# Spectral filter and squared-ReLU layer on one core: seven products for the first group too, a casting load of W_out, and batch 1's filter products moved to slots 12 to 28

## The chip, the cores and the metric

The kernel runs on one core of a Trainium2 chip. A core has TensorE (PE, the matmuls; PEld is its weight load), VectorE (DVE), ScalarE (ACT), GpSimd (POOL) and SyncE (SP), and each runs its own instructions in the order in which the program gives them. Transfers are queued by SP (hardware queue) and by POOL (software queue) and done by 16 DMA engines. The metric is the device time of a whole execution in microseconds, as the median of several runs; the profile is of one execution and has a span of its own, which lies some 2 to 3 us under the measured time.

## The reference, cut to what matters

```python
X = np.fft.rfft(x, axis=1)                       # x: (8, 3008, 256) float32
Y = X * (filt_r + 1j * filt_i)[None]             # filters: (1505, 256)
y = np.fft.irfft(Y, n=3008, axis=1).astype(np.float32)
t = y.reshape(8 * 3008, 256)                     # 24064 tokens
h = np.maximum(t @ w_in, 0.0)                    # w_in: (256, 2048)
return (h * h @ w_out).astype(np.float32)        # w_out: (2048, 256)
```

## The kernel before

The transform is done as matmuls, batch by batch, with two passes through DRAM (`dU` after the first stage, `dZ` after the inverse's first stage). The tokens are worked off in 47 groups of 512. A group takes eight **slots**; in slot s = 8g + k the kernel does one eighth of group g's first matmul (`ffn_g1`, ReLU on ScalarE, square on VectorE) and one eighth of the second matmul of group g - 1. The transform of later batches is laid into the slots by a plan.

The loop, and the plan for batch 1 (the transform of batch 0 is done ahead of the loop, and so is `unit_a` of batch 1):

```python
    for s in range((NG + 1) * SLOTS):
        g, k = divmod(s, SLOTS)
        if g < NG:
            ffn_g1(g, k)                      # 4 matmuls of 512 columns, ReLU
        run(work, s, 0)                       # the plan, first half of the slot
        if 10 <= s < 14:
            make_t(s - 10)                    # sums of blocks of W_out, VectorE
        if (s - 1) // SLOTS - 1 in SEVEN:     # before: groups 1 to 45
            products((s - 1) // SLOTS - 1, (s - 1) % SLOTS)
        if g > 0 and g - 1 not in SEVEN:      # before: groups 0 and 46
            ffn_g2(g - 1, k)                  # 8 matmuls of 256 columns
        run(work, s, 1)
        ...                                   # [cut: ffn_out]
        if g - 1 in SEVEN:
            sums(g - 1, k)                    # VectorE, for k = 0, 1, 2, 4
        if g < NG:
            ffn_sq(g, k)                      # VectorE, every second slot

    # in the plan, for b == 1 (f = 0):
        for k in range(4):
            moves.append(((4.5, 5.5, 7.5, 7.5)[k], cast_wout, k, nc.vector))
        moves.append((0, read_u, b))
        ...                                   # [cut]
        for p in range(12):
            r = 8 + 20 * p / 11 if b == 1 else ...
            units.append((f + r, unit_b, b, p))
            if b == 1 and 2 <= p < 10:
                moves.append((f + r, load_x, 2, p - 2))
            units.append((f + r + (4.5 if b == 1 else ...), unit_p, b, p))
```

The second matmul comes in two forms. `ffn_g2` is the plain one: 64 matmuls of 256 columns a group. `products` splits the matrices into 2 x 2 blocks and takes seven block products in place of eight: 112 matmuls of 128 columns a group, for which VectorE makes four sums of blocks of the squared h (`sums`), and four sums of blocks of W_out once (`make_t`); ScalarE copies four results out and VectorE adds three times.

```python
    def make_t(k):            # b11 .. b22: blocks of sWout
        i0, i1 = ((b12, b11), (b22, t[:, 0]), (b22, b12), (b21, t[:, 1]))[k]
        nc.vector.tensor_sub(out=t[:, k], in0=i0, in1=i1)

    def unit_b(b, p):         # forward transform of two classes, times the filter
        ps = psF(...)                         # a PSUM tag of two buffers
        for i in range(2):
            nc.tensor.matmul(ps[:, i * D:(i + 1) * D], sSB[:, 2 * p + i, :],
                             uts[b][:, 2 * p + i, :], start=True, stop=True)
        nc.vector.tensor_mul(out=prod, in0=..., in1=sF[:, :, 2 * p:2 * p + 2, :])
        for i in range(2):                    # second half added by DMA
            nc.gpsimd.dma_start(out=prod[64 * i:64 * i + 64, 0],
                                in_=prod[64 - 64 * i:128 - 64 * i, 1], accum_op=add)
```

W_out is loaded in float32 through the SP queue between the first two z tiles, into a tile of the two-buffer pool `p_h2`, which the h tiles of the groups use as well; VectorE casts it in four parts in slots 4 to 7. Ahead of the loop:

```python
    read_z(0, 0)
    load_wout(0)          # 1 MB each, nc.sync.dma_start
    read_z(0, 1)
    load_wout(1)
    for c in range(4):
        unit_a(1, c)      # ends in two writes of dU through SP
    for n in range(4):
        unit_y(0, n)      # needs z tile 0
    read_z(0, 2)
```

Of the kernel before, what the change touches and what calls it, by code (L numbers as in the profile page):

```python
# [9 lines left out]
F16 = mybir.dt.float16  # L10
F32 = mybir.dt.float32
# [99 lines left out]
def kernel(  # L111
# [9 lines left out]
    nc = tc.nc  # L121
# [3 lines left out]
    NJT = DFF // 128  # L125
    assert S == N1 * N2 and NF == S // 2 + 1 and D == 256 and DFF == 2048
    T = B * S
    NG = T // TG
# [8 lines left out]
    const = ctx.enter_context(tc.tile_pool(name="const", bufs=1))  # L137
# [9 lines left out]
    p_h2 = ctx.enter_context(tc.tile_pool(name="p_h2", bufs=2))  # L147
# [152 lines left out]

    sWin = const.tile([128, 2, DFF], F16, name="sWin")
    sWout = const.tile([128, NJT, 256], F16, name="sWout")
    w32s = {}

    def load_win():

# [12 lines left out]
    wins = []  # L319

    def load_wout(k):
        if k == 0:
            w32s[2] = p_h2.tile([128, NJT, 256], F32, tag="h2", name="wout32")
        c = slice(8 * k, 8 * k + 8)
        nc.sync.dma_start(out=w32s[2][:, c, :],
                          in_=moe_w_out.rearrange("(jt r) c -> r jt c", r=128)[:, c, :])

    def cast_wout(k, eng):
        c = slice(4 * k, 4 * k + 4)
        eng.tensor_copy(out=sWout[:, c, :], in_=w32s[2][:, c, :])  # L330


    def write_u(b, c):
# [144 lines left out]
    ztiles = [const.tile([112, 8, D], F16, name=f"zt_{c}") for c in range(2)]  # L478
# [3 lines left out]
    def read_z(b, c, ks=(0, 1)):  # L482
        zt = ztiles[c % 2]
        v = dZ[b].rearrange("(q j) d -> q j d", j=NM)
        for k in ks:
            nc.sync.dma_start(out=zt[64 * k:64 * k + 48],
                              in_=v[48 * k:48 * k + 48, 8 * c:8 * c + 8, :])
        zts[(b, c)] = zt
# [29 lines left out]
    def ffn_g1(g, s):  # L518
        if s == 0:
            h2s[g] = p_h2.tile([128, NJT, TG], F16, tag="h2", name=f"h2_{g}")  # L520
        h2 = h2s[g]
        ps = psH(f"psH_{g}_{s}")
        segs = []
        t = g * TG
        while t < (g + 1) * TG:
            b, r = divmod(t, S)
            n = min((g + 1) * TG - t, S - r)
            segs.append((t - g * TG, b, r, n))
            t += n
        for i in range(2):  # L530
            jt = 2 * s + i
            for o, b, r, n in segs:
                for dt in range(2):
                    nc.tensor.matmul(ps[:, i, o:o + n],  # L534
                                     sWin[:, dt, jt * 128:(jt + 1) * 128],
                                     yts[b][:, dt, r:r + n],
                                     start=(dt == 0), stop=(dt == 1))
        nc.scalar.activation(out=h2[:, 2 * s:2 * s + 2, :], in_=ps, func=AF.Relu)  # L538
# [8 lines left out]
    def ffn_g2(g, s):  # L547
        t, half = divmod(s, 2)
        if s % 4 == 0:
            pso[g] = psO(f"psO_{g}_{s}")  # L550
        elif g == NG - 1 and half == 0:
            pso[g] = psF(f"psO_{g}_{s}").rearrange("p (a d) -> p a d", d=256)
        for jt in range(8 * half, 8 * half + 8):
            nc.tensor.matmul(pso[g][:, t % 2, :], h2s[g][:, jt, t * 128:(t + 1) * 128],  # L554
                             sWout[:, jt, :], start=(jt == 0), stop=(jt == NJT - 1))
# [36 lines left out]
    def make_t(k):  # L592

        w = sWout.rearrange("p (q e) c -> p q e c", e=2)
        b11, b12 = w[:, :, 0, 0:128], w[:, :, 0, 128:256]
        b21, b22 = w[:, :, 1, 0:128], w[:, :, 1, 128:256]
        if k == 0:
            sg["t"] = p_t.tile([128, 4, 8, 128], F16, tag="t", name="sT")
        t = sg["t"]
        i0, i1 = ((b12, b11), (b22, t[:, 0]), (b22, b12), (b21, t[:, 1]))[k]  # L600
        nc.vector.tensor_sub(out=t[:, k], in0=i0, in1=i1)
        sg["w"] = {1: b11, 2: b21, 3: b22, 4: t[:, 3], 5: t[:, 0], 6: t[:, 1], 7: t[:, 2]}
# [70 lines left out]
    def fft_plan():  # L673

        fixed, units, moves = [], [], []
        for b in range(1, B):
            f = (b * S // TG) * SLOTS - (48 if b > 1 else 40)
            d = 0
            if b == 1:
                for n in range(4, 16):  # L680
                    fixed.append(((n if n < 8 else n + 2 if n < 12 else 2 * n - 7) + n % 2 / 2,
                                  unit_y, 0, n))
                moves.append((7.5, read_z, 0, 3))
                for k in range(4):
                    moves.append(((4.5, 5.5, 7.5, 7.5)[k], cast_wout, k, nc.vector))
                moves.append((0, read_u, b))
                d = 7
            else:
                for a in range(16):
                    if a % 2 == 0 and b > 2:  # L690
                        moves.append((f + ((-57 + 2.3 * a) if b == 3 else (-66 + 2.75 * a)),
                                      load_x, b, a // 2))
                    if a % 4 == 3:
                        units.append((f + ((-13, -9, -5.5, -3)[a // 4], -46 + 2.1 * a, -56 + 2.75 * a)[min(b, 4) - 2],
                                      unit_a, b, a // 4))
                moves.append((f + (2 if b == 2 else -6.5), read_u, b))
            for p in range(12):
                r = 8 + 20 * p / 11 if b == 1 else 6 + 28 * p / 11 if b == 2 else -2 + 36 * p / 11
                units.append((f + r, unit_b, b, p))
                if b == 1 and 2 <= p < 10:  # L700
                    moves.append((f + r, load_x, 2, p - 2))
                units.append((f + r + (4.5 if b == 1 else 7 - 2.5 * p / 11), unit_p, b, p))
            for c in range(4):
                moves.append((f + (40 + d / 14, 43, 48, 54)[c] - d, read_z, b, c))
            for n in range(16):
                (fixed if n < 4 else units).append((f + YN[n] - d, unit_y, b, n))
        work, used, done = {}, set(), {}
        for r, *u in fixed:
            h = int(2 * r)
            used.add(h)  # L710
            work.setdefault(h, []).append(u)
        rank = (unit_a, unit_b, unit_p, unit_y)
        for r, *u in sorted(units, key=lambda u: (rank.index(u[1]), u[0])):
            after = done.get((u[0], u[1]), -1)
            if u[0] is unit_a:
                h = min((h for h in range(max(2 * int(r) - 2, after + 1), 2 * int(r) + 12)
                         if h % 2 == 0 and not used & {h - 1, h, h + 1}),
                        key=lambda h: abs(h - 2 * r))
                used |= {h - 1, h, h + 1}
                done[(u[0], u[1])] = h  # L720
                work.setdefault(h, []).append(u)
                continue
            early = 1 if u[0] is unit_b else 3
            h = min((h for h in range(max(int(2 * r) - early, after + 1), int(2 * r) + 12)
                     if h not in used),
                    key=lambda h: (sum(h + i in used for i in (-2, -1, 1, 2)) > 2) * 2
                    + abs(h - int(2 * r)))
            used.add(h)
            done[(u[0], u[1])] = h
            work.setdefault(h, []).append(u)  # L730
        for r, *u in moves:
            work.setdefault(int(2 * r), []).append(u)
        return work

    def run(plan, s, place):
        for f, *a in plan.get(2 * s + place, ()):
            f(*a)
# [10 lines left out]
    for k in range(2):  # L748
        c = slice(12 * k, 12 * k + 12)
# [24 lines left out]
    for k in range(6):  # L774
        if k % 3 == 0:
            sSPx.append(p_u.tile([128, 12, 128], F16, tag="u", name=f"sSPx_{k}"))
        c, o = slice(4 * k, 4 * k + 4), slice(4 * k % 12, 4 * k % 12 + 4)
# [6 lines left out]
    for k in range(7):  # L784
# [7 lines left out]
        if k < 4:  # L792
            place_f(0, k + 2, nc.scalar)
    read_z(0, 0)
    load_wout(0)
    read_z(0, 1)
    load_wout(1)
    for c in range(4):
        unit_a(1, c)
    for n in range(4):  # L800
# [1 line left out]
    prologue[0] = False  # L802
    read_z(0, 2)

    SEVEN = range(1, NG - 1)
    work = fft_plan()

    for s in range((NG + 1) * SLOTS):
        g, k = divmod(s, SLOTS)
        if g < NG:  # L810
            ffn_g1(g, k)
        run(work, s, 0)
        if 10 <= s < 14:
            make_t(s - 10)
        if (s - 1) // SLOTS - 1 in SEVEN:
            products((s - 1) // SLOTS - 1, (s - 1) % SLOTS)
        if g > 0 and g - 1 not in SEVEN:
            ffn_g2(g - 1, k)
        run(work, s, 1)
        if g > 0 and g - 1 not in SEVEN:  # L820
            ffn_out(g - 1, k)
        if g - 1 in SEVEN:
            sums(g - 1, k)
        if g < NG:
            ffn_sq(g, k)
# [30 lines left out]
```

## Time and profile before

| what | value |
|---|---|
| time, median of 3 runs | 764.76 us (764.64 to 764.91) |
| span of the profiled execution | 761.6 us |
| TensorE busy | 741.7 us, 97% of the span |
| VectorE busy | 653.3 us, 86% |
| ScalarE busy | 564.5 us, 74% |
| TensorE idle, 0 to 50 us / 50 to 76 us / 76 to 700 us | 8.5 / 5.1 / 2.8 us |

The last row is what matters for this change: it is read from the busy time of TensorE in these stretches. The loop of slots begins near 50 us. A wait is found in the table of who waited for whom, and its place in the timeline of the engine. Busy times of one instruction on VectorE overlap a little: the elementwise operations of 1.22 us follow one another at 1.13 to 1.15 us, so sums over a stretch are taken from start to start.

### The profile page before, as it was taken

How to read it: one execution, taken by the hardware profiler on the slowest of the kernel's cores; microseconds unless marked ns; L12 is line 12 of the kernel's file. 1: busy time of each engine (PE TensorE's matmuls, PEld its weight loads, DVE VectorE, ACT ScalarE, POOL GpSimd, SP SyncE). 2: the span in 40 equal slices, each digit the busy share in tenths (PEclk: the TensorE clock that was granted, in tenths of full speed). 3: DMA queues.
4: the chain of work that ended last, by engine and by line, in shares of the span. 5: the costliest groups of instructions: out<-in, count | busy, mean ns of one | idle time of the engine just before them, and what ended most of it. 6: DMA issues, size and time to landing. Idle time of an engine off the chain costs nothing.

```text
span 761.6 us, 19875 instructions
## 1 busy us (share of the span) xinstructions
PE 741.7 (97%) x8358; PEld 542.3 (71%) x8358; DVE 653.3 (86%) x727; ACT 564.5 (74%) x801; POOL 191.6 (25%) x264
## 2 busy tenths in 40 slices
PE   8977999999999999999999999999999999999998
PEld 5834766777777777877678776787767777777776
DVE  5856987899899998998979999899989989888783
ACT  3965788778877777777777877777777777777773
POOL 3802540143312331233212324033311222000000
PEclk9999999999999999999999999999999999999999
DMA  9986787665776556654585655775546334321011
GB/s 365 300 235 197 126 165 195 181 134 118 151 198 146 104 119 172 184 120 102 125 213 135 123 117 114 199 153 107 110 119 194 90 71 98 97 79 48 29 57 56
DMA packets 103025, 107.54 MB, mean 141 GB/s; under 512 B 10144, under 2 KB 93472, under 8 KB 101400
## 3 DMA queue, kind: packets, MB, share of 16 engines
q1 hardware_dynamic: 85576, 84.09, 36.4%
q0 software_dynamic: 17216, 22.00, 20.4%
q8 instruction: 65, 1.06, 0.6%
q10 hardware_dynamic: 144, 0.18, 0.1%
q14 instruction: 24, 0.20, 0.1%
HBM read 57.97 MB, written 48.23 MB: 139 GB/s over the span
## 4 chain that ended last, share of the span: by engine, by line
PE 87%; DMA 6%; DVE 3%; ACT 2%; SPq 1%; issue 1%; POOL 0%; DVEq 0%; ACTq 0%
PE psH L534 39%; PE psX L647 20%; PE psY L647 15%; PE psY L504 3%; PE psB L423 2%; PE psP L468 2%; DMA f<-in_filt_i_dram 2%; PE psO L554 2%; PE psA L355 2%; DVE prod L431 1%; SPq L338 1%; DMA zt<-dZ 1%; DMA prod<-prod 1%; DMA dZ<-ze 1%; DVE h L545 1%
## 5 line engine op out<-in xcount | busy, mean ns | idle before, releaser
L538 ACT ACTIVATE h<-psH 128x1024 f16<-128x1024 f32 x376 | 385.5, 1026 | 167.8 <-PE psH L534 164.0
L534 PE MATMUL psH<-yt,sWin 128*128 128x512 f16 (+7 forms) x1728 | 388.0, 352 | 1.2 <-ACT h L538 0.5
L545 DVE TENSOR_TENSOR h<-h 128x2048 f16<-128x2048 f16 (+1 forms) x192 | 229.9, 1198 | 46.8 <-ACT h L538 46.4
L438 POOL DMA_DIRECT2D prod<-prod x168 | 138.6, 962 | 441.4 <-DVE prod L431 438.8
L534 PEld LDWEIGHTS <-sWin 128*128 128x128 f16 x1728 | 149.4, 98 | 91.3 <-issue 4.3
L647 PEld LDWEIGHTS <-sum 128*128 128x128 f16 x2880 | 177.4, 98 | 25.2 <-issue 5.3
L647 PEld LDWEIGHTS <-h 128*128 128x128 f16 x2160 | 132.6, 98 | 24.4 <-issue 5.3
L431 DVE TENSOR_TENSOR prod<-psB,sF 128x1024 f16<-128x1024 f32 x84 | 102.5, 1220 | 18.6 <-PE psB L423 17.5
L647 PE MATMUL psX<-sT,sum 128*128 128x128 f16 x1440 | 102.4, 219 | 0.0
L647 PE MATMUL psY<-sT,sum 128*128 128x128 f16 x720 | 69.7, 219 | 0.0
L195 POOL DMA_DIRECT2D x<-in_x_dram x64 | 55.3, 1030 | 2.2 <-PE psA L355 2.2
L623 DVE TENSOR_TENSOR sum<-sum,h 128x2048 f16<-128x2048 f16 x45 | 54.9, 1221 | 0.9
L647 PE MATMUL psY<-sWout,sum 128*128 128x128 f16 x720 | 54.7, 219 | 0.6 <-DVE bot L662 0.6
L647 PE MATMUL psY<-sWout,h 128*128 128x128 f16 x720 | 55.0, 219 | 0.0
L647 PE MATMUL psX<-sT,h 128*128 128x128 f16 x720 | 54.9, 219 | 0.0
L629 DVE TENSOR_TENSOR sum<-h,sum 128x2048 f16<-128x2048 f16 x45 | 54.8, 1218 | 0.0
L626 DVE TENSOR_TENSOR sum<-h 128x2048 f16<-128x2048 f16 x45 | 54.8, 1217 | 0.0
L620 DVE TENSOR_TENSOR sum<-h 128x2048 f16<-128x2048 f16 x45 | 54.7, 1215 | 0.0
L470 ACT CAST ze<-psP 128x512 f16<-128x512 f32 x84 | 49.1, 585 | 0.7 <-PE psP L468 0.4
L647 PE MATMUL psX<-sWout,h 128*128 128x128 f16 x720 | 47.6, 219 | 0.0
L504 PE MATMUL psY<-sC,zt 112*128 112x94 f16 x512 | 43.1, 207 | 3.5 <-DMA zt<-dZ 3.2
L513 DVE CAST yt<-psY 128x376 f16<-128x376 f32 x62 | 33.7, 543 | 14.2 <-PE psY L504 14.2
(75 smaller groups left out, 583.3 us busy)
## 6 DMA issues: line engine op xcount, KB each, us to landing
zt<-dZ SPq DMA_DIRECT2D x64, 192.0 KB
dU<-u SPq DMA_DIRECT2D x56, 192.0 KB
prod<-prod POOLq DMA_DIRECT2D x168, 64.0 KB, 2.7
dZ<-ze SPq DMA_DIRECT2D x28, 384.0 KB
x<-in_x_dram POOLq DMA_DIRECT2D x48, 192.0 KB, 5.0
ut<-dU SPq DMA_DIRECT2D x7, 1024.0 KB
out_dram<-top SPq DMA_DIRECT2D x31, 128.0 KB
out_dram<-bot SPq DMA_DIRECT2D x31, 128.0 KB
```

The source lines that it names most:

```text
L195: nc.gpsimd.dma_start(out=t[64 * h + p0:64 * h + p1], in_=v[p0:p1, 8 * c:8 * c + 8, :])
L431: nc.vector.tensor_mul(out=prod, in0=ps.rearrange("p (a d) -> p a d", d=D).unsqueeze(1).to_broadcast([128, 2, 2, D]), in1=sF[:, :, 2 * p:2 ...
L438: nc.gpsimd.dma_start(out=prod[64 * i:64 * i + 64, 0], in_=prod[64 - 64 * i:128 - 64 * i, 1], accum_op=mybir.AluOpType.add)
L504: nc.tensor.matmul(ps[:, 94 * jj:94 * jj + 94], zt[:, 4 * (g % 2) + jj, dt * 128:(dt + 1) * 128], sSY, start=True, stop=True)
L534: nc.tensor.matmul(ps[:, i, o:o + n], sWin[:, dt, jt * 128:(jt + 1) * 128], yts[b][:, dt, r:r + n], start=(dt == 0), stop=(dt == 1))
L538: nc.scalar.activation(out=h2[:, 2 * s:2 * s + 2, :], in_=ps, func=AF.Relu)
L545: nc.vector.tensor_mul(out=v, in0=v, in1=v)
L620: nc.vector.tensor_add(out=t, in0=a21, in1=a22)
L623: nc.vector.tensor_sub(out=t, in0=f[5], in1=a11)
L626: nc.vector.tensor_sub(out=t, in0=a11, in1=a21)
L629: nc.vector.tensor_sub(out=t, in0=a12, in1=f[6])
L647: nc.tensor.matmul(o[:, t, :], f[p][:, q, 128 * t:128 * t + 128], sg["w"][p][:, q, :], start=(m == 0 and p in (1, 2)), stop=(q == 7), skip ...
```

## The change

Four things are moved or replaced. W_out is loaded by POOL's queue with a cast to float16 in the transfer, straight into its final tile; its start is tied to the arrival of the first z tile by a one-element copy on GpSimd. The four casts on VectorE and the float32 tile go. Group 0's second matmul takes the seven products instead of the plain form, which needs the sums of W_out two slots earlier, in slots 8 to 11. Batch 1's filter products (`unit_b`, and `unit_p` and the loads of batch 2's x with them) start in slot 12 and not in slot 8, and lie closer together. The purpose is to keep the transfers that the first slots wait for free of W_out, and to give TensorE other work while batch 1's transformed rows are still under way.

```diff
     def load_wout(k):
-        if k == 0:
-            w32s[2] = p_h2.tile([128, NJT, 256], F32, tag="h2", name="wout32")
         c = slice(8 * k, 8 * k + 8)
-        nc.sync.dma_start(out=w32s[2][:, c, :],
-                          in_=moe_w_out.rearrange("(jt r) c -> r jt c", r=128)[:, c, :])
-
-    def cast_wout(k, eng):
-        c = slice(4 * k, 4 * k + 4)
-        eng.tensor_copy(out=sWout[:, c, :], in_=w32s[2][:, c, :])
+        nc.gpsimd.dma_start(out=sWout[:, c, :],
+                            in_=moe_w_out.rearrange("(jt r) c -> r jt c", r=128)[:, c, :])
@@ the plan
-                for k in range(4):
-                    moves.append(((4.5, 5.5, 7.5, 7.5)[k], cast_wout, k, nc.vector))
@@
-                r = 8 + 20 * p / 11 if b == 1 else 6 + 28 * p / 11 if b == 2 else -2 + 36 * p / 11
+                r = 12 + 16.5 * p / 11 if b == 1 else 6 + 28 * p / 11 if b == 2 else -2 + 36 * p / 11
@@ ahead of the loop
     read_z(0, 0)
-    load_wout(0)
     read_z(0, 1)
-    load_wout(1)
+    tiny = const.tile([1, 1], F16, name="tiny")
+    nc.gpsimd.tensor_copy(out=tiny, in_=ztiles[0][0:1, 0, 0:1])
+    for k in range(2):
+        load_wout(k)
@@ the loop
-    SEVEN = range(1, NG - 1)
+    SEVEN = range(NG - 1)
@@
-        if 10 <= s < 14:
-            make_t(s - 10)
+        if 8 <= s < 12:
+            make_t(s - 8)
```

More of the change, by code (lines that the diff above doesn't have):

```diff
@@ L302 @@
     sWout = const.tile([128, NJT, 256], F16, name="sWout")
-    w32s = {}
     def load_win():
```

## The prediction

> **What bounds the kernel now.** I read the page first: its shares say which engine is short of time.
>
> ```profile
> PE 741.7 (97%) x8358; PEld 542.3 (71%) x8358; DVE 653.3 (86%) x727; ACT 564.5 (74%) x801; POOL 191.6 (25%) x264
> ```
>
> TensorE is the bound over the whole; what it doesn't lose early it keeps to the end, because from 140 to 700 us it has under 1.5 us of idle time. So the change can only pay where TensorE stands still or runs slowly, and the table of who waited for whom, taken for TensorE from 40 to 130 us, names the places:
>
> ```profile
> PE psB L423 <- DMA ut<-dU: 4.1, 1, 4.1
> PE psY L504 <- DMA zt<-dZ: 3.2, 2, 2.8
> PE psA L355 <- DVE prod L431: 0.7, 1, 0.7
> ```
>
> The first is the largest wait of the whole trace: the first filter product of batch 1 waits for batch 1's rows. TensorE's timeline shows where it lies, and what follows it (start us, length us):
>
> ```profile
> 60.27 0.81 PE L534 MATMUL psH<-yt,sWin 128*128 128x512 f16 x3 [0.34 <-DVE yt L513]
> 65.15 0.61 PE L423 MATMUL psB<-ut,sSB 128*128 128x256 f16 x2 [4.08 <-DMA ut<-dU]
> 65.56 1.91 PE L554 MATMUL psO<-sWout,h 128*128 128x256 f16 x8
> ```
>
> 60.27 is slot 8. TensorE stands from 61.1 to 65.15. The SP queue says why the rows are late:
>
> ```profile
> 44.92 0.39 SPq L325 DMA_DIRECT2D wout<-in_moe_w_out_dram x1
> ...
> 46.44 0.43 SPq L325 DMA_DIRECT2D wout<-in_moe_w_out_dram x1
> 46.97 10.49 SPq L338 DMA_DIRECT2D dU<-u  x8
> 57.57 1.38 SPq L486 DMA_DIRECT2D zt<-dZ  x2
> 61.29 0.82 SPq L414 DMA_DIRECT2D ut<-dU x2
> ```
>
> The eight writes of dU take 10.49 us to issue although their data stand ready, with 2 MB of W_out queued ahead of them; only then can ut be read. The stretches around it (length, busy us of PE, PEld, DVE, ACT, POOL, granted clock, DMA share, GB/s):
>
> ```profile
> 61.10:65.15 4.05, 0.00 (x0) 0.00 (x1) 1.45 (x2) 1.02 (x1) 0.00 (x0) 0.95 0.71 231
> 65.15:68.60 3.45, 3.45 (x15) 2.05 (x16) 1.23 (x1) 0.00 (x0) 1.27 (x2) 0.56 0.93 303
> 68.60:84.30 15.70, 15.59 (x121) 10.83 (x120) 13.44 (x15) 11.54 (x15) 7.96 (x12) 1.00 0.51 85
> 84.30:107.40 23.10, 22.26 (x246) 15.92 (x246) 22.34 (x23) 18.02 (x28) 13.22 (x19) 1.00 0.83 152
> ```
>
> Two things to see. After the stall the granted clock is 0.56 for 3.45 us. And from 84.3 to 107.4 us VectorE is busy 22.34 of 23.1 us: there it has as little room as TensorE.
>
> **What the Trainium skill says.** "TensorE: Matmul & The Clock Gate", Part 1, says that after an idle window of some 3.4 us the array's clock falls to half, and needs about as long of steady work to come back. The trace agrees: 4.05 us idle, then 0.56 for 3.45 us. "DMA: Bandwidth & Descriptors", section on queues, rings and completion order, says that each DMA engine goes round robin between the queues it has work for; so W_out in POOL's queue will share with the dU writes and not stand ahead of them. The trace before can't show it for this stage. The same page, section "SWDGE vs HWDGE vs iDMA", says that a cast in a transfer goes by the software queue only; the x loads here do so (192 KB of output land in 5.0 us, median). "SBUF — State Buffer", in the "DVE blocks DMA" box, says that VectorE in a two-port mode keeps GpSimd from writing descriptors; nothing before shows whether the squares would delay W_out so.
>
> **The change part by part.**
>
> *The wait for ut.* Without W_out ahead, dU's 1.5 MB and ut's first 0.5 MB need less queueing. In the old run 44 to 60 us moved some 300 GB/s. Shared half and half with W_out, I estimate dU done near 57, ut's first part near 62 and the second near 64. The first product now stands in slot 12 to 13, near 68 us. So the 4.05 us are gone, with some 5 us in hand.
>
> *The clock.* 3.45 us at 0.56 are 1.93 us of work at full clock: 1.5 us saved, as TensorE no longer idles long enough.
>
> *Seven products for group 0.* The chain of waits has 8 plain matmuls in 0.87 us and 16 block products in 0.90 us at full clock. 64 x 0.109 = 6.96 us go, 112 x 0.056 = 6.27 us come: 0.7 us saved on TensorE. On TensorE alone the sum is 4.05 + 1.5 + 0.7 = 6.2 us.
>
> *VectorE pays.* Group 0 now needs four sums (1.15 us start to start) and three adds (0.34 us): 4.6 + 1.0 = 5.6 us, all before slot 17 and so in front of batch 1's last products. The four casts of W_out (2.7 us) go, but they lay in slots 4 to 7, where the ReLUs at 1.02 us on ScalarE set the pace; they free nothing that counts. The built order has the same 12 products up to slot 28 as before. In the old run VectorE went from 62.5 (last square of group 0) to 108.9 us (end of the twelfth product): 46.4 us, of which 7.9 idle in the rows of that stretch, 6.2 of it on those products' matmuls. That leaves 38.5 us of work. After the change it is 38.5 + 5.6 = 44.1 us, from 61.6 on (the ReLU of slot 7 ends at 60.4, the square takes 1.2). It ends at 105.7 against 108.9: **3.2 us** earlier, not 6.2.
>
> *How far TensorE may be ahead.* The twelfth product's matmul needs a buffer of the tag psF. The one two allocations before is the half of psA that VectorE copies; after that copy VectorE still has a square and two products, 3 x 1.14 = 3.4 us. So TensorE can reach it at 105.7 - 3.4 = 102.3 us against 107.4: 5.1 us earlier. The next inverse product waits for the eleventh product's buffer, which costs some 0.4 us. I take 4.7 us. From there to the end the work is the same as before, and VectorE has room again (16.53 of 20.1 us busy from 107.4 to 127.5), so the gain stays.
>
> *W_out itself.* It is first needed in slot 8 (first sum, VectorE) and slot 9 (first block product), near 61.5 us. It starts when z tile 0 is there, near 47.5. Its 2.1 MB read at half of 300 GB/s take 14 us, at the full rate 7; dU's writes finish in between, so I put its landing at 58 to 62. Some 0.3 us of expected loss.
>
> *Sum.* 764.8 - 4.7 + 0.3 = 760.4; I choose **760.3 us**, a little lower as h's second tile no longer waits for W_out's casts (1.1 us on ScalarE in slot 8, off TensorE's path before only because of the stall).
>
> **The rivals.**
>
> *A. TensorE keeps it all.* VectorE's extra 5.6 us hide, as sums are wanted only two slots after they are made. For it: TensorE is the chain from 65 to 96 us in the old run. Against it: VectorE had 96.7% from 84.3 to 107.4 us already, before anything was added. Time: 764.8 - 6.2 = 758.6.
>
> *B. W_out comes late.* If the software queue is slower than its half, sums and block products wait in order on both engines. Landing at 65 gives the old stall back under another name (sT or psX waiting for sWout), and a slow clock again. For it: W_out starts 2.6 us later than before and shares. Against it: the old run moved the same bytes by 61.3 us through one queue, W_out first. Time: 763 to 765.
>
> *C. The z tile of batch 1.* The last inverse product moves from the end of slot 32 to slot 33. In the old run z of batch 1 was read just in time: TensorE waited 0.37 us at 127.5. A later write turns part of the gain into that wait. It would cost 0.5 to 1.5 us: 761 to 762. Against it: the SP queue held that write back by stores until 121.42, while its tile was ready at 117.5, so there is room.
>
> **Range and chances.** VectorE's bound gives 3.2 to 5.1 us, TensorE's 6.2, a late W_out near 0, and the z wait takes up to 1.5. Eight in ten I put between 757.8 and 763.3. 2% are 15.3 us; no term comes near that, as TensorE has only 5.1 us idle from 50 to 76 us. So within 2% has 0.98, and each side 0.01.
>
> **What would show it.** Right: no wait of psB for ut; granted clock at 1.0 from 61 to 69 us; L325 and the cast's line gone; VectorE over 95% busy from slot 9 to slot 28, and the waits of TensorE there name it (psB, psP or psA behind prod); slot 28's products 4 to 5 us earlier. Wrong: sWout named in a wait near 61 us (B); psY waiting for zt over 1 us near 122 (C); VectorE with gaps of some us between 70 and 105 while TensorE is closed up (A). The prediction fails most if the software queue takes over 16 us for W_out, or if dU's writes stay slow to issue without it.

## The result, and the profile after

The changed kernel takes **759.2 us** (758.92 to 759.70) against 764.84 us for the kernel before on the same chip: a ratio of 0.9924, 95% interval 0.9906 to 0.9941. It is faster by about 0.8%, and lies within 2%, inside the predicted range and 1.1 us under the predicted 760.3.

The page's first lines hardly move: TensorE 741.7 to 740.7 us busy, VectorE 653.3 to 655.8. What moved is seen only in the first 130 us. Who waited for whom, TensorE, 40 to 130 us, in the changed kernel (us in total, times, longest):

```profile
PE psY L497 <- DMA zt<-dZ: 3.4, 2, 3.1
PE psB L416 <- DVE prod L424: 1.0, 1, 1.0
PE psY L640 <- DVE bot L655: 0.8, 1, 0.8
...
PE psP L461 <- DVE prod L424: 0.5, 1, 0.5
PE psY L497 <- DVE prod L424: 0.4, 2, 0.2
```

The wait of psB for ut is gone. The first line was there before; in place of the long wait stand the short ones below it, and they name VectorE. The stretches from slot 8 on (length, busy us of PE, PEld, DVE, ACT, POOL, granted clock, DMA share, GB/s) say the same:

```profile
61.00:65.00 4.00, 3.90 (x40) 2.60 (x40) 3.59 (x6) 3.06 (x5) 0.00 (x0) 1.00 0.37 99
65.00:69.00 4.00, 4.00 (x54) 3.05 (x52) 4.00 (x6) 2.78 (x4) 0.00 (x0) 1.00 1.06 402
69.00:84.00 15.00, 13.04 (x137) 9.13 (x134) 14.97 (x18) 9.35 (x15) 7.81 (x10) 1.00 0.44 81
84.00:103.00 19.00, 18.52 (x203) 13.17 (x202) 18.55 (x20) 14.85 (x23) 13.12 (x18) 1.00 0.94 160
```

TensorE works through where it stood from 61.1 to 65.15, at full clock. From 65 to 84 us VectorE is busy 18.97 of 19 us and TensorE only 17.04: the bound has passed from a transfer to VectorE. The SP queue, though, hardly changed:

```profile
45.66 10.16 SPq L331 DMA_DIRECT2D dU<-u  x8
55.93 1.74 SPq L479 DMA_DIRECT2D zt<-dZ  x2
62.56 0.82 SPq L407 DMA_DIRECT2D ut<-dU  x2
```

The dU writes still take 10.16 us to issue (10.49 before), and ut is read at 62.56 us, later than the 61.29 of before. W_out left the SP queue and the rows came no sooner. In the other nine traces with the casting load the writes took 8.5 to 9.6 us, but ut was read at 61.7 to 64.0 us, so it was never sooner than before.

In the two traces the first inverse unit of batch 1 (slot 38) starts at 127.55 us before and at 124.46 us after, 3.1 us apart:

```profile
127.55 0.33 PE L504 MATMUL psY<-sC,zt 112*128 112x94 f16 x4 [0.37 <-DMA zt<-dZ]
```

```profile
124.46 0.33 PE L497 MATMUL psY<-sC,zt 112*128 112x94 f16 x4 [0.33 <-DMA zt<-dZ]
```

Another 0.9 us is a wait of an inverse product for its addition near 364 us, which of these two only the trace before has. Together they are the 4.0 us between the spans. The medians differ by 5.6 us: the profiled execution of before took 763.72 us, 1.1 under its median, and the changed kernel's 759.70, 0.5 over. Between 200 and 700 us TensorE is idle for 0.6 to 1.9 us in five of the fourteen traces of this study and not at all in the other nine, so the traces are used for places and causes, the medians for sizes.

The wait near 364 us may not be chance. The three kernels that load W_out as before (before, e1, e3) all have it, at 0.7 to 1.1 us; of the ten with the casting load none has, but e11, which loads nothing, has 0.6 us of it. Each is one execution, and no run shows what causes it.

### The profile page after: what moved, and what is told of

The parts are those of the page before. It is cut to its first block, busy times and chain, and to the rows that moved or that the text cites. A ratio compares the mean times of both kernels' runs of the same rounds, so it can differ in the third digit from the quotient of the medians.

```text
span 757.6 us, 19976 instructions
## 1 busy us (share of the span) xinstructions
PE 740.7 (98%) x8406; PEld 542.3 (72%) x8406; DVE 655.8 (87%) x730; ACT 564.7 (75%) x803; POOL 193.9 (26%) x267
## 4 chain that ended last, share of the span: by engine, by line
PE 87%; DVE 5%; DMA 4%; ACT 2%; issue 1%; SPq 0%; DVEq 0%; ACTq 0%
PE psH L527 40%; PE psX L640 20%; PE psY L640 16%; PE psY L497 3%; PE psB L416 2%; PE psP L461 2%; DMA f<-in_filt_i_dram 2%; PE psA L348 2%; DVE prod L424 2%; ACT h L531 1%; PE psO L547 1%; DVE h L538 1%; DMA zt<-dZ 1%; DMA dZ<-ze 1%; PE psf L284 1%
## 5 line engine op out<-in xcount | busy, mean ns | idle before, releaser
L640 PEld LDWEIGHTS <-sum 128*128 128x128 f16 x2944 | 181.4, 98 | 26.2 <-issue 6.3
L640 PEld LDWEIGHTS <-h 128*128 128x128 f16 x2208 | 135.6, 98 | 24.5 <-issue 5.3
L640 PE MATMUL psX<-sT,sum 128*128 128x128 f16 x1472 | 104.7, 219 | 0.0
L619 DVE TENSOR_TENSOR sum<-h 128x2048 f16<-128x2048 f16 x46 | 56.0, 1217 | 0.0
L613 DVE TENSOR_TENSOR sum<-h 128x2048 f16<-128x2048 f16 x46 | 55.9, 1216 | 0.0
```

Source lines behind the costliest of these rows:

```text
L613: nc.vector.tensor_add(out=t, in0=a21, in1=a22)
L619: nc.vector.tensor_sub(out=t, in0=a11, in1=a21)
L640: nc.tensor.matmul(o[:, t, :], f[p][:, q, 128 * t:128 * t + 128], sg["w"][p][:, q, :], start=(m == 0 and p in (1, 2)), stop=(q == 7), skip ...
```

## The experiments

All were compared with the kernel before on their own chip.

**e1: the move alone.** The kernel before with `r = 12 + 16.5 * p / 11` for batch 1.

```diff
-                r = 8 + 20 * p / 11 if b == 1 else ...
+                r = 12 + 16.5 * p / 11 if b == 1 else ...
```

> The kernel before with one edit: batch 1's filter products from slot 12 on. My theory (the gain comes from the move, W_out's new way does nothing for the transfers of dU and ut): the wait of psB for ut (4.1 us) and the half clock after it (1.5 us) go; VectorE has only its old 38.5 us from 62.5 on and ends the twelfth product near 101 to 104, so TensorE sets the end: 5 to 5.5 us less, 759.3 to 760. Rival (W_out's way out of the SP queue is what pays): the move alone leaves most of the loss, 762 to 764.

Measured 760.23 against 764.67 us, ratio 0.9936 (0.9924 to 0.9949). The theory holds, though the time is 0.2 us above the 759.3 to 760 that it gave: one line gives 4.4 us. The wait for ut isn't in the list of waits, while ut is still read at 61.05 us. The interval overlaps that of the changed kernel (0.9906 to 0.9941). The line also packs the products closer and takes the loads of batch 2's x with it; e12 below, with the same packing from slot 11, speaks for the start as what counts.

**e2: W_out alone.** The kernel before with only the casting loads and the one-element copy. The edits shown undo the rest in the changed kernel.

```diff
-                r = 12 + 16.5 * p / 11 if b == 1 else ...
+                r = 8 + 20 * p / 11 if b == 1 else ...
-    SEVEN = range(NG - 1)
+    SEVEN = range(1, NG - 1)
-        if 8 <= s < 12:
-            make_t(s - 8)
+        if 10 <= s < 14:
+            make_t(s - 10)
```

> The kernel before with W_out by casting loads behind the first z tile, nothing else. My theory: ut still comes at 64 to 66 us as dU's writes are as slow to issue as before (10.2 us in the changed kernel against 10.5), so the wait of psB for ut stays at 4 us or a little more: 764 to 766. Rival (W_out's way pays): ut comes before slot 8, the wait goes, 759 to 761.

Measured 764.47 against 764.67 us, ratio 1.0001 (0.9993 to 1.0010): nothing. Its SP queue and TensorE's wait:

```profile
45.73 9.32 SPq L331 DMA_DIRECT2D dU<-u  x8
55.16 1.89 SPq L479 DMA_DIRECT2D zt<-dZ  x2
62.28 0.82 SPq L407 DMA_DIRECT2D ut<-dU  x2
```

```profile
PE psB L416 <- DMA ut<-dU: 4.1, 1, 4.1
```

The dU writes were issued by 55.05, 2.4 us sooner than in the kernel before, yet ut could be read only at 62.28, when their data had landed. The chains of work that ended last show the landing of the last write, first in the kernel before, then in e2:

```profile
56.51 4.70 DMA dU<-u
61.29 3.82 DMA ut<-dU
```

```profile
53.59 8.55 DMA dU<-u
62.28 3.64 DMA ut<-dU
```

The last write was issued 2.9 us earlier, took 3.9 us longer, and landed at 62.14 in place of 61.21. Out of the queue is not out of the way.

**e3: seven products for group 0 alone**, with the sums of W_out in slots 8 to 11 (the two edits that e2 undoes, made in the kernel before).

> The kernel before with seven products for group 0 and the sums of W_out in slots 8 to 11, nothing else. Theory A (VectorE is the bound from 70 to 107 us, so its 5.6 us more cost more than TensorE's 0.7 us less): 766 to 769. Theory B (TensorE is the bound, the sums hide): 764.0 to 764.5.

Measured 765.49 against 764.67 us, ratio 1.0010 (1.0001 to 1.0020): slower, though the interval only just clears 1, so theory A's direction, but by 0.8 us and not by the 1.3 to 4 it gave. The wait for ut was still there (3.6 us), and part of VectorE's extra work lay in it: VectorE was idle 2.5 us for the products' matmuls in 61 to 107 us, where the kernel before had 6.2.

**e4: the changed kernel without the seven products for group 0** (SEVEN and `make_t` undone as in e2).

> The changed kernel with the plain second matmul for group 0 and the sums of W_out back in slots 10 to 13. Theory A (VectorE bound by the sums of group 0): the twelfth product ends near 101 to 103 instead of 106.9, TensorE sets the end: 756.5 to 758.5. Theory B (TensorE bound): 0.7 us more than the changed kernel, 759.7 to 760.2.

Measured 758.73 against 764.67 us, ratio 0.9913 (0.9899 to 0.9926). Theory B had it 0.7 us above the changed kernel, and it isn't; but against 0.9924 and 0.9931 for the changed kernel on other chips the intervals overlap, so e4 alone doesn't decide. Its list of waits shows what took over:

```profile
PE psY L497 <- DMA zt<-dZ: 4.2, 2, 2.7
PE psP L461 <- DMA prod<-prod: 0.7, 1, 0.7
```

With VectorE relieved, TensorE comes to slot 38 early and waits 1.5 us there for batch 1's z (0.33 in the changed kernel). The twelfth product ended at 105.07 us, not at the 101 to 103 expected.

e4 and e1 differ only in W_out's way; e4's ratio is lower by 0.0023, with intervals that touch. By slot 38 e1 is the earlier of the two (122.96 against 123.73 us), and what e1 loses comes later: its trace has 1.9 us of waits between 200 and 700 us, one of them the wait near 364 us above, and e4's has none. Whether the casting load helps once the move is made stays open.

**e5: the changed kernel again**, for comparison on the next chip.

> The changed kernel itself, so that the others of this call are compared with it on one chip: 759.2 as before (758.9 to 759.7), the same waits.

Measured 759.41 against 764.84 us, ratio 0.9931 (0.9918 to 0.9943).

**e6: the changed kernel with the products back from slot 8.**

```diff
-                r = 12 + 16.5 * p / 11 if b == 1 else ...
+                r = 8 + 20 * p / 11 if b == 1 else ...
```

> The changed kernel with batch 1's filter products back from slot 8 on. Theory (the move is what pays): ut is read at 62.6 us in the changed kernel, so a first product in slot 8 waits for it until about 66.5; psB waits 4 to 5 us for ut, and group 0's seven products then press VectorE as well: 764.5 to 767. Rival (the three other parts pay a good share): 761 to 763.

Measured 765.65 against 764.84 us, ratio 1.0019 (1.0009 to 1.0028). Without the move the other three parts together cost 0.8 us:

```profile
PE psB L416 <- DMA ut<-dU: 4.3, 1, 4.3
PE psY L497 <- DMA zt<-dZ: 3.6, 2, 3.0
PE psY L497 <- DVE prod L424: 2.1, 2, 1.9
```

**e7: the clock.** In the changed kernel's trace the granted clock stays at half until 54 us, around the 3.1 us wait for z tile 0; in e5's trace of the same kernel it is back by 52. This version keeps TensorE busy through that wait.

```diff
-            for k in range(2):
+            for k in range(46 if n == 0 else 2):
+                k %= 2
                 nc.tensor.matmul(ps[:, 128 * k:128 * k + 128], zero, zero, start=True, stop=True)
```

> The changed kernel with 44 more zero matmuls of 128 columns in front of the first inverse unit, while TensorE waits for z tile 0 (44.6 to 47.9 us), their results overwritten. Theory: the granted clock stays at 1.0 and the first slots run at full clock, so the first ReLU comes 1.5 us earlier than 52.0 and slot 8 1 to 2 us earlier than 61.1; VectorE starts slot 8 earlier by as much: 757.2 to 758.2. Rival: W_out's arrival or the z tiles hold slot 8 at 61 anyway, and nothing is gained (759.2), or the extra matmuls delay the first unit (759.5).

Measured 759.02 us beside e5's 759.41; ratios 0.9926 (0.9914 to 0.9939) and 0.9931: not to be told apart. Yet the clock did stay up. First the stretch of the changed kernel again (e5), then of e7:

```profile
50.00:52.00 2.00, 1.98 (x7) 0.70 (x6) 0.30 (x1) 0.37 (x1) 0.00 (x0) 0.68 1.17 181
```

```profile
50.00:52.00 2.00, 1.75 (x9) 0.73 (x8) 0.00 (x0) 1.78 (x2) 0.00 (x0) 1.00 1.25 172
```

The ReLU of slot 8 starts at 59.59 us, 1.4 earlier than e5's 60.99. Then e7 waits 0.9 us for z tile 2 and VectorE 0.5 us for W_out, and 0.7 us for z in slot 38: the time went into new waits for transfers.

**e8: batch 2's x loads earlier**, on e4.

```diff
-                    moves.append((f + r, load_x, 2, p - 2))
+                    moves.append((f + 12 + (p - 2) / 2, load_x, 2, p - 2))
```

> The changed kernel with the plain second matmul for group 0 (as in e4) and with batch 2's x loads in slots 12 to 15.5, not spread between the additions by DMA up to slot 25. Theory C (with VectorE relieved, the additions queued on GpSimd behind the x loads are what TensorE waits for): the waits of psP for prod and x go, 0.5 to 1.5 us less than e4: 757.2 to 758.3. Rival (z of batch 1 at slot 38 takes the gain back, as e4's 1.5 us wait of psY for zt shows): psY waits longer instead and the time is e4's, 758.7.

Measured 760.09 against 764.84 us, ratio 0.9934 (0.9921 to 0.9946). No gain over e4's 0.9913 (0.9899 to 0.9926): theory C falls. The wait of psP for prod grew (1.4 us) and psY's for zt stayed (5.0 us in all, 1.4 of it in slot 38).

**e9 and e10: z of batch 1 out of the stores' way.** Both have e7's zero matmuls and this edit; e9 has the plain second matmul for group 0, e10 the seven products.

```diff
         if i6 == 2:
-            nc.sync.dma_start(
+            (nc.scalar if (b, c) == (1, 3) else nc.sync).dma_start(
```

> The plain second matmul for group 0 (e4), the zero matmuls of e7, and the last write of batch 1's z issued from ScalarE's queue instead of SP's, where it stands behind six stores. Theory C (z of batch 1 at slot 38 is what took back the gains of e4, e7 and e8): the wait of psY for zt near 123 us goes and the time falls to 756 to 757.5. Rival (something after slot 38 levels all versions): 758.5 to 759.5 as before.

> The same with the seven products for group 0, so the changed kernel with e7's zero matmuls and the z write moved. Theory A (VectorE is the bound in slots 8 to 28 when group 0 takes seven products): 1 to 2 us slower than e9, 757.5 to 758.5. Theory B (TensorE bound): 0.7 us faster than e9.

Measured on one chip (764.09 before): e9 **757.07** us, ratio 0.9906 (0.9892 to 0.9919); e10 758.75 us, ratio 0.9922 (0.9908 to 0.9935). The medians are 1.7 us apart, in the direction and of the size that theory A gave; the intervals still overlap a little, and e3 and e4 point the same way. VectorE between 70 and 107 us, first e9, then e10:

```profile
70.00:107.00 37.00, 35.86 (x367) 25.52 (x365) 36.20 (x36) 28.06 (x42) 24.32 (x34) 1.00 0.82 146
```

```profile
70.00:107.00 37.00, 34.31 (x373) 24.61 (x371) 36.51 (x38) 26.57 (x41) 22.68 (x32) 1.00 0.78 142
```

With seven products VectorE is a little fuller and TensorE 1.55 us less busy: its waits there name VectorE (0.9 us for a product, 0.8 us for an add). The wait in slot 38 is not gone (0.9 us in e9), as the read of z still stands in the SP queue behind the stores; it is e4's 1.5 that became smaller, while a new wait of 1.0 us for W_out came up near 62 us. e9's interval overlaps e4's, so a gain from moving the z write, theory C, is not shown. e9 beats the changed kernel in its median by some 2 us, with overlapping intervals.

**e11: no W_out at all.** The load is left out and its tile filled with zeros near the start, so the output is zero; one run.

```diff
-        nc.gpsimd.dma_start(out=sWout[:, c, :],
-                            in_=moe_w_out.rearrange("(jt r) c -> r jt c", r=128)[:, c, :])
+        pass
```

> The changed kernel without the load of W_out at all: its tile is filled with zeros on VectorE near the start, so the output is zero and 2 MB of reads are left out. Theory D (W_out's transfer crowds the DMA engines whichever queue it uses, so that dU's writes and ut come late): the eight writes of dU issue in 5 to 7 us instead of 10.2, and ut is read before 58 us instead of 62.6. Rival (dU's writes are slow by themselves, 512 bytes at a time): they still take 9 to 10 us and ut is read after 60. In both the time is about 759 or a little less, as ut isn't waited for.

```profile
45.93 6.55 SPq L331 DMA_DIRECT2D dU<-u  x8
52.59 1.55 SPq L479 DMA_DIRECT2D zt<-dZ  x2
55.31 0.82 SPq L407 DMA_DIRECT2D ut<-dU  x2
```

Theory D holds: without W_out the writes issue in 6.55 us and ut is read 7.3 us earlier. W_out holds dU up in either queue. The one run took 759.94 us, no less than the changed kernel: with the products in slot 12, ut's earlier arrival gains nothing.

**e12: one slot earlier**, on e9 (`r = 11 + 16.5 * p / 11`).

> The best version so far (plain second matmul for group 0, zero matmuls, z write from ScalarE's queue) with batch 1's filter products one slot earlier, from slot 11. Theory C (what is left is the 0.9 us wait of psY for zt in slot 38): z is ready a slot, some 2 us, earlier, the wait goes, and the time is 0.5 to 1 us under e9: 756.1 to 756.6. Rival (ut, read at 63.2 us, is not there by slot 11, near 66 us): psB waits 0.5 to 1.5 us for ut and the time is 757 to 758.5.

Measured 759.59 against 764.16 us, ratio 0.9937 (0.9923 to 0.9950): the rival was right, and the loss is larger than it gave; the interval lies clear of e9's (0.9892 to 0.9919). The profiled execution was the slowest of the five. TensorE's timeline:

```profile
64.06 1.04 PE L548 MATMUL psO<-sWout,h 128*128 128x256 f16 x8
66.69 0.54 PE L416 MATMUL psB<-ut,sSB 128*128 128x256 f16 x2 [1.59 <-DMA ut<-dU]
67.02 1.91 PE L528 MATMUL psH<-yt,sWin 128*128 128x512 f16 x4
68.73 1.75 PE L548 MATMUL psO<-sWout,h 128*128 128x256 f16 x8
```

With the 1.6 us wait the half clock came back: eight matmuls of 256 columns take 1.75 us where 1.04 stands at full clock. Slot 11 is too early for ut; nothing between 11 and 12 was tried.

## Why the prediction was right, and where it was off

**The wait for ut: the right result by a wrong step.** The 4.05 us went, but the working had dU done near 57 us and ut arriving at 62 to 64, "5 us in hand". In the changed kernel ut was read only at 62.56, when dU had landed. In e12 and e2 it arrived 3.6 to 3.7 us after that issue, which puts it near 66.3 here (an estimate); the first product started at 70.15, so somewhat under 4 us were in hand, 2 of them because the product itself came later than the "near 68 us" of the working. The step that failed is "W_out will share with the dU writes and not stand ahead of them", taken to mean that they would be done sooner. The Trainium skill ("DMA: Bandwidth & Descriptors", queues, rings and completion order) says that engines go round robin between queues, and the runs fit that; but ut must wait for the last write, and with the engines shared the last write landed no sooner than before (62.14 us in e2, 61.21 before). e1, e2 and e6 show what paid: the move alone gives 4.4 us, and without it the other parts give nothing.

**The clock: right after slot 8** (1.00 from 61 to 69 us), and not foreseen before it: in this trace the cold stretch around z tile 0 lasted until 54 us, and the last square of group 0 ended 1.1 us later than the 61.6 assumed for it. In e5, where the cold stretch ended by 51.5, that square ended at 61.7. e7 shows the clock to be of little worth by itself.

**Seven products: VectorE pays, as the working had it.** VectorE's lines in the changed kernel, the last square of group 0, the first sum, and the last two products:

```profile
61.46 1.23 DVE L538 TENSOR_TENSOR h<-h 128x2048 f16<-128x2048 f16 x1 [0.41 <-ACT h L531]
62.61 0.69 DVE L594 TENSOR_TENSOR sT<-sWout 128x1024 f16<-128x1024 f16 x1
...
104.59 2.35 DVE L424 TENSOR_TENSOR prod<-psB,sF 128x1024 f16<-128x1024 f32 x2
```

From 62.7 to 106.9 us are 44.2 us, predicted 44.1. Only the start was off by the 1.1 us above, so the end was at 106.9 and not 105.7. Rival A falls with this. e3, e4 and the pair e9 and e10 agree that the seven products for group 0 took back some of the move's gain, by the medians 0.5 to 1.7 us; only e3's interval is clear of no difference, so the direction is well supported and the size stays open.

**TensorE's lead was over-sized.** The twelfth product's matmul starts at 104.15, where the lead of 3.4 us promised 102.3: the lead was 2.8 us from that start to VectorE's end, behind an end that came 1.2 later. So at slot 28 the trace shows 3.1 us (104.15 against 107.26), not 4.7. The medians' 5.6 us came out above the 4.5 predicted and not below it: 0.9 us of that is the wait near 364 us in the trace before and the rest the runs' spread, neither of which the working had; to that extent the right number is luck.

**W_out's arrival, rival B: at the edge as said.** It started at 45.80 us, not near 47.5, as the one-element copy reads only the part of z tile 0 that the first of its two transfers brings. It landed 13.8 us after its second issue, at 60.5 us, just in time for 62.6; e5 waited 0.4 us for it, e9 1.0 us.

**Rival C** cost 0.33 us in the changed kernel and was thus no worse than before. It grew in the versions that keep the plain form for group 0: 1.2 us in e1, 1.5 in e4.

## What to carry to other kernels

When a consumer waits for a transfer that is late for good reasons, giving it other work first can be worth more than all work on the transfer: one line of the plan gave 4.4 us, the new way for W_out by itself nothing. Moving a load to another queue does not take its bytes off the engines; leaving it out in a trial shows what it costs its neighbours. Before trading one engine's work for another's, sum both engines' work over that very stretch: the seven products take less TensorE time than the plain form (by the working's estimate 0.7 us a group), but in a stretch where VectorE was 97% busy they lose.

## What was not expected of the hardware

A wait of 1.6 us, with two short gaps of 0.23 and 0.46 us in the 5 us ahead of it (e12), was enough for the clock to fall to half until 70 us. The Trainium skill ("TensorE: Matmul & The Clock Gate", Part 1) speaks of an idle window of some 3.4 us that runs freely; here less idle time sufficed.

After much the same wait for z tile 0 (3.1 and 2.9 us) the half clock lasted to 54 us in one trace of the changed kernel and to 51.5 in another. Added up over stretches of half a microsecond, the time at half clock comes out as 3.4 us or as 6.8 us in each of fifteen cases and never between. Around the wait for z tile 0 it was 3.4 us in before, e1, e5, e6 and e8 and 6.8 us in the changed kernel, e2, e3, e4 and e11; around the later wait for ut it was 3.4 us in before, e3, e6 and e12 and 6.8 us in e2. That is one or two windows of the length that the page gives. Half of that time is lost, so much the same wait can cost an estimated 1.7 us of work in one execution and 3.4 us in another.

Matmuls of zeros held the clock up through the wait (e7: 1.00 from 44 us on).
